# Rebuilding the opening of a fused recurrence and max-out kernel: block 0 transposed in fp32, weights in quarters, gate scale in the drive term, block 0's sums held open, TensorE warmed

## The chip, the cores and the metric

The kernel runs on one core of one Trainium2 chip. The metric is device microseconds of one execution; smaller is better. A run over 1.5% above the fastest of its kernel is called slow below, and kernels are compared by their fast runs. Times within a trace count from the start of its span, which is about 1.8 us shorter than the time of the run.

PE is TensorE, PEld its weight loads, DVE VectorE, ACT ScalarE, POOL GpSimd, SP SyncE (SPq its queue of DMA issues). A number like L381 is a line of that kernel's own source, so the same work has different line numbers in different kernels.

## The reference

```python
# x, f_logit: (4, 6144, 256); lower_bound: (256,); w1, w2: (256, 1024); w_out: (1024, 256)
sig = 1.0 / (1.0 + np.exp(-f_logit))
f = lower_bound + (1.0 - lower_bound) * sig
i = 1.0 - f
for t in range(S):                      # a recurrence over the sequence, per channel
    h = f[:, t] * h + i[:, t] * x[:, t]
    y[:, t] = h
tokens = y.reshape(B * S, D)            # 24576 x 256
out = np.maximum(tokens @ w1, tokens @ w2) @ w_out
```

Two identities matter. With om = 1 - lower_bound and u = sigmoid(-f_logit), i = om * u, and om is a constant of the channel. And max(a, b) = a + relu(b - a), so out = y @ (w1 @ w_out) + relu(y @ (w2 - w1)) @ w_out. The kernel calls w2 - w1 `wd` and w1 @ w_out `w13`.

## The kernel before

The 24576 tokens are worked in 48 blocks of 512. For each block f_logit and x are brought to channels-on-partitions, either by TensorE transposes (the first four blocks) or by a transposing DMA out of a bf16 scratch (all others, in chunks of two blocks: `fT`, `xT`). ACT makes u; DVE makes the decay ff, the drive v = u * x, and two scans of 512 columns, which give y. TensorE then does the first layer (16 matmuls of 512 columns with `wd`, each pair followed by a relu on ACT) and the second layer (40 matmuls of 256 columns: 8 with `w13`, 32 with `w_out`, called `wob`). In the loop the two layers of neighbouring blocks are interleaved. The part in question is what comes ahead of that loop:

```python
# block 0 comes in two halves of 256 tokens: cast to bf16, transpose, recurrence
        first_bf16(0, 0, nc.vector.tensor_copy)
        first_bf16(0, 1, nc.vector.tensor_copy)
        first_turn(0)
        first_recurrence(0)
        first_bf16(1, 0, nc.scalar.copy)
        first_bf16(1, 1, nc.scalar.copy)
        first_turn(1)
        first_recurrence(1)
        for fc in range(2):
            make_wd(fc, 1)          # w2 - w1 in fp32, then scaled by om into bf16
        make_wd(2, 2)
        pts = [turn_w1(0), turn_w1(1)]
        for fc in range(2):
            first_layer(0, fc)
        # ... (the rest of the first layer of block 0, w1 transposed for w13) ...
        make_w13()                  # scaled by om too: the scans run on u * x, without om
        turn(turn_steps(1))
        recurrence(1)               # gate, decays, drive, scans of block 1
        ahead("cross", cross, 4)
        for fc in range(FC):
            second_layer(0, fc)
        turn(turn_steps(2))
        gate(2)
        for fc in range(FC):
            first_layer(1, fc)
        for step in scan_steps(2):
            step()
        steps = turn_steps(3)
        turn(steps)
        if steps:
            gate(3)
        # ... the loop over blocks 2 to 47 ...

        def drive():                # for both halves of the channels at once
            xT = turned[j, 1]
            nc.vector.tensor_tensor(
                out=like(v[:, :, 0:nb], xT),
                in0=like(u[:, :, 0:nb], xT),
                in1=xT,
                op=ALU.mult,
            )
```

The weights are fetched in halves of 512 KB, w2 ahead of w1.

## Time and profile before

| | before |
|---|---|
| runs before the prediction, us | 402.15, 400.65, 424.38 |
| the profiled execution, us | 428.3 (a slow one) |
| first useful matmul of the weights, us | 11.2 |
| first layer of block 1 begins, us | 27.25 |
| a block in the loop, us | 7.82 |

How to read it: the profile that was there before the prediction is of a slow execution. The windows view tells what of it is the slow state. Its columns are the stretch, its length, then the busy time of PE, PEld, DVE, ACT and POOL with the number of instructions, the granted clock of TensorE, the DMA share and GB/s.

```profile
40.50:428.00 387.50, 360.19 (x2514) 273.36 (x2557) 219.89 (x312) 246.68 (x407) 18.55 (x39) 0.99 1.03 174
```

From 40.5 us on, TensorE worked 360.2 of 387.5 us. The waits view (who waited for whom: us in total, times, longest) says for what: the sigmoids waited 35.5 us for transposing DMAs.

```profile
ACT u L190 <- DMA fT<-scr_1_91: 18.2, 7, 4.6
ACT u L190 <- DMA fT<-scr_0_90: 17.3, 8, 5.2
```

40.5 + 360.2 = 400.7 us, which is within 2 us of the spans of the two later traces of this kernel outside the slow state (400.0 and 398.8 us). So a fast run has next to no stall in the loop, and only the opening offers time. Its timeline (start, duration, engine, line, operation, count, and in brackets the idle time just before with what ended it):

```profile
11.18 1.95 PE L352 MATMUL psO<-ident_f,w1n_110 128*128 128x128 f32 x8 [3.44 <-DMA w1n_110<-in_moe_w_dram]
12.93 3.62 PE L381 MATMUL dT<-y,wd 128*128 128x512 bf16 x8
...
17.63 1.89 PE L381 MATMUL dT<-y,wd 128*128 128x512 bf16 x7
...
21.75 1.02 ACT L190 ACTIVATE u<-tT 128x1024 bf16<-128x1024 bf16 x1
...
24.59 2.46 DVE L233 TENSOR_TENSOR_SCAN y<-ff,y,v 128x512 bf16<-128x512 bf16 x2
...
26.96 1.26 DVE L430 COPY osb<-psO 128x512 f32<-128x512 f32 x2
...
27.25 3.93 PE L381 MATMUL dT<-y,wd 128*128 128x512 bf16 x15
...
28.14 0.61 DVE L209 TENSOR_SCALAR ff<-u,nom 128x512 bf16<-128x512 bf16 x2
```

TensorE waits for the first half of w1 until 11.2 us. Its first eight first-layer matmuls run 0.43 us apart, the later ones 0.216. Block 1's first layer (L381 at 27.25) follows its scans (L233) directly.

### The profile page before, as it was taken

To read this page: it belongs to the slowest core of one execution; us is meant where nothing else is said; L and a number is where in the kernel's file an instruction comes from. 1 tells how busy PE (TensorE), PEld (TensorE's weight loads), DVE (VectorE), ACT (ScalarE), POOL (GpSimd) and SP (SyncE) were. 2 spreads that over 40 slices of the span, in tenths; PEclk is the share of its full clock that TensorE was granted. 3 is DMA by queue.
4 is the path that set the end of the run, shared out by engine and by line. 5 is a ranking of instruction groups with operands and counts; after the bars stand their busy time and mean duration, and the time that the engine had idled before them with its cause. 6 is when DMAs were issued, how large, how long until landed. Compare 5 with 4: busy or idle time off the path is not lost.

```text
span 428.3 us, 6970 instructions
## 1 busy us (share of the span) xinstructions
PE 392.8 (92%) x2744; PEld 296.8 (69%) x2792; DVE 248.7 (58%) x359; ACT 268.5 (63%) x447; POOL 26.4 (6%) x58
## 2 busy tenths in 40 slices
PE   3999979798789999998997899999998999999996
PEld 1677756576557777776775577767676777777775
DVE  5785637455357566564653557657547656567551
ACT  3656656557366676675673666756657676776762
POOL 1400000000000000000000000000000000000000
PEclk9999999999989999999999699999999999999999
DMA  7999999999999999999998999999999999998112
GB/s 245 222 220 198 123 157 141 137 169 252 81 240 226 119 239 233 112 248 168 183 237 75 218 158 186 250 145 170 219 131 231 226 216 164 268 157 179 79 69 100
DMA packets 103377, 77.01 MB, mean 180 GB/s; under 512 B 93552, under 2 KB 94064, under 8 KB 102640
## 3 DMA queue, kind: packets, MB, share of 16 engines
q1 hardware_dynamic: 100512, 51.13, 66.7%
q0 software_dynamic: 2544, 25.17, 36.1%
q8 instruction: 22, 0.36, 0.4%
q10 hardware_dynamic: 288, 0.26, 0.2%
q14 instruction: 11, 0.09, 0.1%
HBM read 53.48 MB, written 48.23 MB: 237 GB/s over the span
## 4 chain that ended last, share of the span: by engine, by line
PE 46%; DMA 34%; SPq 15%; ACT 3%; DVE 1%; issue 1%; ACTq 0%
PE psO L410 25%; DMA fT<-scr_0_90 20%; PE dT L381 19%; SPq L153 13%; DMA fT<-scr_1_91 12%; ACT u L190 2%; DMA w1n_110<-in_moe_w_dram 2%; SPq L433 1%; PE psO L352 1%; ACT rt L389 1%; PE tT L180 1%; PE psO L365 0%; SPq L121 0%; DVE osb L430 0%; DVE y L233 0%
## 5 line engine op out<-in xcount | busy, mean ns | idle before, releaser
L389 ACT ACTIVATE rt<-dT 128x512 bf16<-128x512 f32 x384 | 219.2, 598 | 104.1 <-PE dT L381 100.0
L381 PE MATMUL dT<-y,wd 128*128 128x512 bf16 x720 | 219.5, 384 | 21.3 <-ACT rt L389 19.5
L410 PE MATMUL psO<-wob,rt 128*128 128x256 bf16 x1536 | 230.7, 274 | 2.7 <-issue 0.4
L410 PEld LDWEIGHTS <-rt 128*128 128x128 bf16 x1536 | 170.7, 114 | 41.4 <-issue 1.1
L233 DVE TENSOR_TENSOR_SCAN y<-ff,y,v 128x512 bf16<-128x512 bf16 x88 | 107.9, 1268 | 0.1
L430 DVE COPY osb<-psO 128x512 f32<-128x512 f32 x94 | 64.7, 690 | 59.0 <-PE psO L410 58.9
L381 PEld LDWEIGHTS <-wd 128*128 128x128 bf16 x768 | 75.8, 99 | 33.2 <-issue 24.6
L209 DVE TENSOR_SCALAR ff<-u,nom 128x512 bf16<-128x512 bf16 x94 | 29.0, 351 | 105.0 <-ACT u L190 105.0
L410 PE MATMUL psO<-w_109,y 128*128 128x256 bf16 x384 | 74.0, 275 | 0.0
L410 PEld LDWEIGHTS <-y 128*128 128x128 bf16 x384 | 43.4, 113 | 42.6 <-issue 3.5
L190 ACT ACTIVATE u<-fT 128x1024 bf16<-128x1024 bf16 x44 | 46.4, 1054 | 35.5 <-DMA fT<-scr_1_91 18.2
L220 DVE TENSOR_TENSOR v<-u,xT 128x1024 bf16<-128x1024 bf16 x44 | 30.3, 688 | 3.8 <-DMA xT<-scr_0_92 1.8
L98 POOL DMA_DIRECT2D scr_0_90<-in_f_logit_dram x11 | 5.4, 493 | 149.7 <-DMA fT<-scr_0_90 149.7
L98 POOL DMA_DIRECT2D scr_1_91<-in_f_logit_dram x11 | 5.3, 486 | 148.8 <-DMA fT<-scr_1_91 148.1
L233 DVE TENSOR_TENSOR_SCAN y<-ff,v 128x512 bf16<-128x512 bf16 x6 | 7.0, 1208 | 0.0
L98 POOL DMA_DIRECT2D scr_0_92<-in_x_dram x11 | 5.4, 488 | 18.7 <-DMA xT<-scr_0_92 16.9
L98 POOL DMA_DIRECT2D scr_1_93<-in_x_dram x11 | 5.3, 486 | 15.7 <-DMA xT<-scr_1_93 14.9
L190 ACT ACTIVATE u<-tT 128x1024 bf16<-128x1024 bf16 x3 | 3.2, 1058 | 4.3 <-PE tT L180 4.3
L352 PE MATMUL psO<-ident_f,w1n_110 128*128 128x128 f32 x8 | 1.9, 422 | 3.4 <-DMA w1n_110<-in_moe_w_dram 3.4
L341 ACT ACTIVATE wd<-wdf,om 128x128 bf16<-128x128 f32 (+1 forms) x6 | 2.2, 428 | 4.3 <-DVE wdf L333 4.3
L352 PEld LDWEIGHTS psO<-ident_f,w1n_110 128*128 128x128 f32 x8 | 1.6, 221 | 3.7 <-issue 3.7
L220 DVE TENSOR_TENSOR v<-u,tT 128x1024 bf16<-128x1024 bf16 x3 | 3.6, 1216 | 0.0
(49 smaller groups left out, 45.1 us busy)
## 6 DMA issues: line engine op xcount, KB each, us to landing
out_dram<-osb SPq DMA_DIRECT2D x47, 512.0 KB, 4.8
scr_0_90<-in_f_logit_dram POOLq DMA_DIRECT2D x11, 512.0 KB, 7.5
scr_0_92<-in_x_dram POOLq DMA_DIRECT2D x11, 512.0 KB, 12.4
scr_1_91<-in_f_logit_dram POOLq DMA_DIRECT2D x11, 512.0 KB, 7.9
scr_1_93<-in_x_dram POOLq DMA_DIRECT2D x11, 512.0 KB, 13.6
fn<-in_f_logit_dram POOLq DMA_DIRECT2D x3, 256.0 KB, 7.9
xn<-in_x_dram POOLq DMA_DIRECT2D x3, 256.0 KB, 8.6
w2n_112<-in_moe_w_dram SPq DMA_DIRECT2D x1, 512.0 KB, 6.5
```

The source lines that it names most:

```text
L98: nc.gpsimd.dma_start(out=scr[0:nt, :].rearrange("(p i) d -> p (i d)", p=P), in_=src.rearrange("(p i) d -> p (i d)", p=P),)
L153: nc.sync.dma_start_transpose(out=dst[:, :, 0:nt], in_=held[c, s][0:nt, :])
L180: nc.tensor.transpose(dst, src, ident[:])
L190: nc.scalar.activation(out=like(u[:, :, 0:nb], fT), in_=fT, func=AF.Sigmoid, scale=-1.0)
L209: nc.vector.tensor_scalar(out=ff[:, h, 0:nb], in0=u[:, h, 0:nb], scalar1=nom[:, h : h + 1], scalar2=1.0, op0=ALU.mult, op1=ALU.add,)
L220: nc.vector.tensor_tensor(out=like(v[:, :, 0:nb], xT), in0=like(u[:, :, 0:nb], xT), in1=xT, op=ALU.mult,)
L233: nc.vector.tensor_tensor_scan(out=y[:, h, 0:nb], data0=ff[:, h, 0:nb], data1=v[:, h, 0:nb], initial=init, op0=ALU.mult, op1=ALU.add,)
L352: nc.tensor.transpose(pt[:, kc, q, :], half(w1n, g)[:, kc, 2 * r + q], ident_f[:])
L381: nc.tensor.matmul(dT[:, 0:nb], lhsT=wd[:, kc, fc * P : (fc + 1) * P], rhs=y[:, kc, 0:nb], start=(kc == 0), stop=(kc == KC - 1),)
L389: nc.scalar.activation(out=rt[:, 0:nb], in_=dT[:, 0:nb], func=AF.Relu)
L410: nc.tensor.matmul(ps[:, r, :], lhsT=left, rhs=right, start=(s == 0 and (r == 0 or j == NBLK - 1)), stop=(s == n - 1 and (r == 1 or j == N ...
L430: nc.vector.tensor_copy(out=osb[:, 2 * g : 2 * g + 2, :], in_=ps[:])
```

## The change

Its intent is to start TensorE earlier and keep it fed:

- block 0's fp32 halves are transposed without the casts to bf16; block 0's decays move from DVE to ACT, and some of its relus from ACT to DVE;
- the weights come in quarters, w1 ahead of w2, so that the first layer can begin on a quarter;
- om goes into the drive (one scaled product for each half of the channels), so `wd` and `w13` need no scaling;
- block 0's second layer begins with the `w_out` part, as soon as its relus are there, and its sums stay open in PSUM until `w13` is ready (`second_first`, `second_last`);
- eight matmuls on a constant are to bring TensorE to its full rate sooner and keep it there (the kernel before had eight small transposes for this);
- half of block 1's second layer is interleaved with block 2's first layer.

The core of the diff (cut):

```diff
-        def drive():
+        def drive(h):
             xT = turned[j, 1]
-            nc.vector.tensor_tensor(
-                out=like(v[:, :, 0:nb], xT),
-                in0=like(u[:, :, 0:nb], xT),
-                in1=xT,
-                op=ALU.mult,
-            )
+            scaled_product(v[:, h, 0:nb], xT[:, h], u[:, h, 0:nb], h)   # x * om * u
...
         return [
             lambda: decay(0),
+            lambda: drive(0),
+            lambda: scan(0),
             lambda: decay(1),
-            drive,
-            lambda: scan(0),
+            lambda: drive(1),
             lambda: scan(1),
         ]
...
-    NG = 2
+    NG = 4
...
+        keep_warm(5)
+        first_turn(0, 0)
+        first_gate(0)
+        first_turn(0, 1)
+        first_drive(0)
+        keep_warm(1)
+        turn_w1(0)
+        first_scan(0, 0)
+        make_wd(0)
+        first_scan(0, 1)
...
+        keep_w1T(1, nc.vector.tensor_copy)
+        keep_w1T(2, nc.scalar.copy)
+        second_first(range(4))
+        keep_w1T(3, nc.vector.tensor_copy)
+        t1 = turn_steps(1)
+        turn(t1[: len(t1) // 2])
+        gate(1)
+        second_first(range(4, 6))
+        turn(t1[len(t1) // 2 :])
+        for step in scan_steps(1):
+            step()
+        second_first(range(6, 8))
         make_w13()
-        turn(turn_steps(1))
-        recurrence(1)
+        turn(turn_steps(2))
+        gate(2)
         ahead("cross", cross, 4)
         for fc in range(FC):
-            second_layer(0, fc)
-        turn(turn_steps(2))
-        gate(2)
-        for fc in range(FC):
             first_layer(1, fc)
+            second_last(fc)
         for step in scan_steps(2):
             step()
         steps = turn_steps(3)
         turn(steps)
-        if steps:
-            gate(3)
+        gate(3)
...
```

More of the change, by code (lines that the diff above doesn't have):

```diff
@@ L115, with fetch_first, first_turn @@
     raws = {}
-    def fetch_first(k):
-        nt = TB // 2
-        for s in range(2):
-            raw = const.tile([P, nt // P, D], FP32, name=f"raw{k}{s}")
-            nc.sync.dma_start(
-                out=raw[:],
-                in_=srcs[s][0, k * nt : (k + 1) * nt, :].rearrange(
-                    "(p i) d -> p i d", p=P
-                ),
-            )
-            raws[k, s] = raw
-    def first_bf16(k, s, copy):
-        raw = raws[k, s]
-        nat = const.tile([P, raw.shape[1], D], BF16, name=f"nat{k}{s}")
-        copy(out=nat[:], in_=raw[:])
-        raws[k, s] = nat
-    def first_turn(k):
-        nt = TB // 2
-        for s in range(2):
-            dst = ps_t.tile([P, KC, nt // P, P], BF16, name="tT")
-            for q in range(nt // P):
-                for h in range(KC):
-                    nc.tensor.transpose(
-                        dst[:, h, q, :],
-                        raws[k, s][:, q, h * P : (h + 1) * P],
-                        ident[:],
-                    )
-            raws[k, s] = dst[:].rearrange("p k i m -> p k m i")
+    HB = TB // 2
+    def fetch_first(k, s):
+        raw = const.tile([P, HB // P, D], FP32, name=f"raw{k}{s}")
+        nc.sync.dma_start(
+            out=raw[:],
+            in_=srcs[s][0, k * HB : (k + 1) * HB, :].rearrange(
+                "(p i) d -> p i d", p=P
+            ),
+        )
+        raws[k, s] = raw
+    def first_turn(k, s):
+        dst = ps_t.tile([P, KC, HB // P, P], FP32, name="tT")
+        for q in range(HB // P):
+            for h in range(KC):
+                nc.tensor.transpose(
+                    dst[:, h, q, :],
+                    raws[k, s][:, q, h * P : (h + 1) * P],
+                    ident_f[:],
+                )
+        raws[k, s] = dst[:].rearrange("p k i m -> p k m i")
     def cross(c):
@@ L195, in like, with scaled_product @@
     def like(t, src):
-        if len(src.shape) == 3:
+        if len(src.shape) == len(t.shape):
             return t
+        if len(t.shape) == 2:
+            return t.rearrange("p (m i) -> p m i", m=P)
         return t.rearrange("p k (m i) -> p k m i", m=P)
+    def scaled_product(out, xT, u, h):
+        nc.vector.scalar_tensor_tensor(
+            out=like(out, xT),
+            in0=xT,
+            scalar=om[:, h : h + 1],
+            in1=like(u, xT),
+            op0=ALU.mult,
+            op1=ALU.mult,
+        )
     def scan_steps(j):
@@ L216, in decay @@
             )
-        def drive():
+        def drive(h):
             xT = turned[j, 1]
-            nc.vector.tensor_tensor(
-                out=like(v[:, :, 0:nb], xT),
-                in0=like(u[:, :, 0:nb], xT),
-                in1=xT,
-                op=ALU.mult,
-            )
+            scaled_product(v[:, h, 0:nb], xT[:, h], u[:, h, 0:nb], h)
         def scan(h):
@@ L250, with first_gate @@
     first = {}
-    def first_recurrence(k):
-        nt = TB // 2
-        cols = slice(k * nt, (k + 1) * nt)
+    def first_gate(k):
+        cols = slice(k * HB, (k + 1) * HB)
         if k == 0:
@@ L258, in first_recurrence @@
             ys[0] = ypool.tile([P, KC, TB], BF16, name="y")
-        u, ff, v, y = (*(first[t] for t in ("u", "ff", "v")), ys[0])
-        fT, xT = raws[k, 0], raws[k, 1]
+        u, ff = first["u"], first["ff"]
+        fT = raws[k, 0]
         nc.scalar.activation(
@@ L264, in first_recurrence, with first_drive, first_scan @@
         for h in range(KC):
-            nc.vector.tensor_scalar(
+            nc.scalar.activation(
                 out=ff[:, h, cols],
-                in0=u[:, h, cols],
-                scalar1=nom[:, h : h + 1],
-                scalar2=1.0,
-                op0=ALU.mult,
-                op1=ALU.add,
-            )
-        nc.vector.tensor_tensor(
-            out=like(v[:, :, cols], xT), in0=like(u[:, :, cols], xT), in1=xT,
-            op=ALU.mult,
-        )
-        for h in range(KC):
-            nc.vector.tensor_tensor_scan(
-                out=y[:, h, cols],
-                data0=ff[:, h, cols],
-                data1=v[:, h, cols],
-                initial=y[:, h, nt - 1 : nt] if k else 0.0,
-                op0=ALU.mult,
-                op1=ALU.add,
-            )
-    def recurrence(j):
-        gate(j)
-        for step in scan_steps(j):
-            step()
+                in_=u[:, h, cols],
+                func=AF.Identity,
+                bias=one[:],
+                scale=nom[:, h : h + 1],
+            )
+    def first_drive(k):
+        cols = slice(k * HB, (k + 1) * HB)
+        for h in range(KC):
+            scaled_product(
+                first["v"][:, h, cols], raws[k, 1][:, h], first["u"][:, h, cols], h
+            )
+    def first_scan(k, h):
+        cols = slice(k * HB, (k + 1) * HB)
+        y = ys[0]
+        nc.vector.tensor_tensor_scan(
+            out=y[:, h, cols],
+            data0=first["ff"][:, h, cols],
+            data1=first["v"][:, h, cols],
+            initial=y[:, h, HB - 1 : HB] if k else 0.0,
+            op0=ALU.mult,
+            op1=ALU.add,
+        )
     ident_f = const.tile([P, P], FP32)
@@ L298 @@
     waited = const.tile([P, 1], FP32)
+    one = const.tile([P, 1], FP32)
+    heat = const.tile([P, TB], BF16)
     warm = const.tile([P, 1], FP32)
     wob = wpool.tile([P, FC, D], BF16)
-    wdf = wpool.tile([P, KC, DFF], FP32)
     wd = wpool.tile([P, KC, DFF], BF16)
@@ L308, with by_unit @@
     w2n = [wpool.tile([P, KC, NQ * P], FP32, name=f"w2n{g}") for g in range(NG)]
-    def half(w, g):
-        return w[g][:].rearrange("p kc (m q) -> p kc q m", q=NQ)
-    def fcs(w, kc, g):
-        return w[:, kc, g * NQ * P : (g + 1) * NQ * P].rearrange(
-            "p (q m) -> p q m", q=NQ
-        )
+    def by_unit(w):
+        return w[:].rearrange("p kc (m q) -> p kc q m", q=NQ)
     def fetch_w(g):
-        cols = slice(g * DFF // NG, (g + 1) * DFF // NG)
-        for w, src in ((w2n, moe_w2), (w1n, moe_w1)):
+        cols = slice(g * NQ * P, (g + 1) * NQ * P)
+        for w, src in ((w1n, moe_w1), (w2n, moe_w2)):
             nc.sync.dma_start(
@@ L324, in fetch_w, with fetch_wo @@
             )
+    def fetch_wo(g, n):
+        rows = slice(g * NQ * P, (g + n) * NQ * P)
+        nc.gpsimd.dma_start(
+            out=wob[:, g * NQ : (g + n) * NQ, :].rearrange(
+                "p (g q) c -> p g (q c)", g=n
+            ),
+            in_=moe_w_out[rows, :].rearrange("(g p q) c -> p g (q c)", g=n, q=NQ),
+        )
     def pool_waits(t):
         nc.gpsimd.tensor_copy(out=waited[:], in_=t)
-    def make_wd(fc, n):
-        g, r = divmod(fc, NQ)
-        qs = slice(r, r + n)
-        cols = slice(fc * P, (fc + n) * P)
-        nc.vector.tensor_tensor(
-            out=wdf[:, :, cols].rearrange("p kc (q m) -> p kc q m", q=n),
-            in0=half(w2n, g)[:, :, qs],
-            in1=half(w1n, g)[:, :, qs],
-            op=ALU.subtract,
-        )
-        for kc in range(KC):
-            if g == 0:
-                nc.scalar.mul(wd[:, kc, cols], wdf[:, kc, cols], om[:, kc : kc + 1])
-            else:
-                nc.vector.tensor_scalar_mul(
-                    out=wd[:, kc, cols], in0=wdf[:, kc, cols], scalar1=om[:, kc : kc + 1]
-                )
@@ L347, in turn_w1, with make_wd @@
-    def turn_w1(k):
-        g, r = divmod(k, NQ // 2)
-        pt = ps_o.tile([P, KC, 2, P], FP32, name="psO")
-        for kc in range(KC):
-            for q in range(2):
-                nc.tensor.transpose(
-                    pt[:, kc, q, :], half(w1n, g)[:, kc, 2 * r + q], ident_f[:]
-                )
-        return pt
-    def keep_w1T(k, pt):
-        dst = w1T[:, 2 * k : 2 * k + 2, :].rearrange("p q (k d) -> p k q d", k=KC)
-        nc.vector.tensor_copy(out=dst, in_=pt[:])
-    def make_w13():
-        for kc in range(KC):
-            psw = ps_o.tile([P, 2, D], FP32, name="psO")
+    def make_wd(g):
+        for kc in range(KC):
+            nc.vector.tensor_tensor(
+                out=wd[:, kc, g * NQ * P : (g + 1) * NQ * P].rearrange(
+                    "p (q m) -> p q m", q=NQ
+                ),
+                in0=by_unit(w2n[g])[:, kc],
+                in1=by_unit(w1n[g])[:, kc],
+                op=ALU.subtract,
+            )
@@ new lines, with turn_w1, keep_w1T, make_w13 @@
+    w1ps = {}
+    def turn_w1(g):
+        pt = ps_o.tile([P, KC, NQ, P], FP32, name="psO")
+        for kc in range(KC):
+            for q in range(NQ):
+                nc.tensor.transpose(
+                    pt[:, kc, q, :], by_unit(w1n[g])[:, kc, q], ident_f[:]
+                )
+        w1ps[g] = pt
+    def keep_w1T(g, copy):
+        dst = w1T[:, NQ * g : NQ * (g + 1), :].rearrange("p q (k d) -> p k q d", k=KC)
+        copy(out=dst, in_=w1ps[g][:])
+    def make_w13():
+        psw = ps_o.tile([P, 2, D], FP32, name="psO")
+        for kc in range(KC):
@@ L364, in make_w13 @@
             for fc in range(FC):
                 nc.tensor.matmul(
-                    psw[:, 0, :],
+                    psw[:, kc, :],
                     lhsT=w1T[:, fc, kc * P : (kc + 1) * P],
                     rhs=wob[:, fc, :],
-                    start=(fc == 0),
-                    stop=(fc == FC - 1),
+                    start=(kc == 0 and fc == 0),
+                    stop=(kc == KC - 1 and fc == FC - 1),
+                    skip_group_check=True,
                 )
-            nc.scalar.mul(w13[:, kc, :], psw[:, 0, :], om[:, kc : kc + 1])
+        nc.scalar.copy(out=w13[:], in_=psw[:])
@@ L374, with relu_act, relu_dve, first_layer @@
     rts = {}
-    def first_layer(j, fc):
-        nb = blocks[j][2]
+    def relu_act(out, in_):
+        nc.scalar.activation(out=out, in_=in_, func=AF.Relu)
+    def relu_dve(out, in_):
+        nc.vector.tensor_scalar_max(out=out, in0=in_, scalar1=0.0)
+    def first_layer(j, fc, relu=relu_act, c0=0, c1=TB):
         y = ys[j]
@@ L381, in first_layer @@
             nc.tensor.matmul(
-                dT[:, 0:nb],
+                dT[:, c0:c1],
                 lhsT=wd[:, kc, fc * P : (fc + 1) * P],
-                rhs=y[:, kc, 0:nb],
+                rhs=y[:, kc, c0:c1],
                 start=(kc == 0),
@@ L387, in first_layer, with second_first, second_last, second_layer @@
             )
-        rt = rpool.tile([P, TB], BF16, name="rt")
-        nc.scalar.activation(out=rt[:, 0:nb], in_=dT[:, 0:nb], func=AF.Relu)
-        rts[j, fc] = rt
+        if c0 == 0:
+            rts[j, fc] = rpool.tile([P, TB], BF16, name="rt")
+        relu(rts[j, fc][:, c0:c1], dT[:, c0:c1])
     acc = {}
-    def second_layer(j, slot):
+    psf = {}
+    def second_first(fcs):
+        ns = TB // P
+        for i in range(ns):
+            g, r = divmod(i, 2)
+            for fc in fcs:
+                if r == 0 and fc == 0:
+                    psf[g] = ps_o.tile([P, 2, D], FP32, name="psO")
+                nc.tensor.matmul(
+                    psf[g][:, r, :],
+                    lhsT=rts[0, fc][:, i:TB:ns],
+                    rhs=wob[:, fc, :],
+                    start=(r == 0 and fc == 0),
+                    stop=False,
+                    skip_group_check=True,
+                )
+    def second_last(k):
+        ns = TB // P
+        i, kc = divmod(k, KC)
+        g, r = divmod(i, 2)
+        if k == 0:
+            psf["osb"] = opool.tile([P, TB // P, D], FP32, name="osb")
+        osb = psf["osb"]
+        nc.tensor.matmul(
+            psf[g][:, r, :],
+            lhsT=ys[0][:, kc, i:TB:ns],
+            rhs=w13[:, kc, :],
+            start=False,
+            stop=(r == 1 and kc == KC - 1),
+            skip_group_check=True,
+        )
+        if r == 1 and kc == KC - 1:
+            nc.vector.tensor_copy(out=osb[:, 2 * g : 2 * g + 2, :], in_=psf[g][:])
+            if g == 1:
+                nc.sync.dma_start(
+                    out=out[0:TB, :].rearrange("(p n) d -> p n d", p=P), in_=osb[:]
+                )
+    def second_layer(j, slot, nslot=FC):
         b, t0, nb, c, o = blocks[j]
@@ L399, in second_layer @@
         total = ns * n
-        for k in range(slot * total // FC, (slot + 1) * total // FC):
+        for k in range(slot * total // nslot, (slot + 1) * total // nslot):
             i, s = divmod(k, n)
@@ L447 @@
     with tc.manual_schedule():
-        nc.sync.dma_start(out=lbc[:], in_=lower_bound.rearrange("(h p) -> p h", p=P))
+        nc.vector.memset(heat[:], 1.0)
+        nc.vector.memset(one[:], 1.0)
+        fetch_first(0, 0)
+        fetch_first(0, 1)
+        nc.scalar.dma_start(
+            out=lbc[:], in_=lower_bound.rearrange("(h p) -> p h", p=P)
+        )
+        fetch_w(0)
+        fetch_first(1, 0)
+        fetch_first(1, 1)
+        for g in range(1, NG):
+            fetch_w(g)
+        nc.scalar.activation(out=warm[:], in_=one[:], func=AF.Sigmoid)
         nc.vector.tensor_copy(out=ident[:], in_=ident_f[:])
@@ L453 @@
         nc.vector.tensor_scalar_add(out=nom[:], in0=lbc[:], scalar1=-1.0)
-        fetch_first(0)
-        fetch_first(1)
-        for g in range(NG):
-            fetch_w(g)
-        pool_waits(w2n[0][:, 0, 0:1])
-        nc.gpsimd.dma_start(
-            out=wob[:].rearrange("p (g q) c -> p g (q c)", g=NG),
-            in_=moe_w_out.rearrange("(g p q) c -> p g (q c)", g=NG, q=NQ),
-        )
+        pool_waits(w2n[1][:, 0, 0:1])
+        fetch_wo(0, 2)
+        fetch_wo(2, 1)
         done["fetch"] = done["cross"] = 1
+        ahead("fetch", fetch, 1)
@@ L464 @@
+        fetch_wo(3, 1)
         ahead("fetch", fetch, 4)
-        nc.scalar.activation(out=warm[:], in_=om[:, 0:1], func=AF.Sigmoid)
-        wt = ps_d.tile([P, TB], BF16, name="dT")
-        for q in range(8):
-            nc.tensor.transpose(wt[:, 0:P], ident[:], ident[:])
-        first_bf16(0, 0, nc.vector.tensor_copy)
-        first_bf16(0, 1, nc.vector.tensor_copy)
-        first_turn(0)
-        first_recurrence(0)
-        first_bf16(1, 0, nc.scalar.copy)
-        first_bf16(1, 1, nc.scalar.copy)
@@ L475 @@
-        first_turn(1)
-        first_recurrence(1)
-        for fc in range(2):
-            make_wd(fc, 1)
-        make_wd(2, 2)
-        pts = [turn_w1(0), turn_w1(1)]
-        for fc in range(2):
-            first_layer(0, fc)
-        for k in range(2):
-            keep_w1T(k, pts[k])
-        for fc in range(2, 4):
-            first_layer(0, fc)
-        make_wd(4, 2)
-        make_wd(6, 2)
-        pts = [turn_w1(2), turn_w1(3)]
-        for fc in range(4, 8):
-            first_layer(0, fc)
@@ L492, with keep_warm @@
-        for k in range(2):
-            keep_w1T(2 + k, pts[k])
+        wt = ps_d.tile([P, TB], FP32, name="dT")
+        def keep_warm(n):
+            for _ in range(n):
+                nc.tensor.matmul(
+                    wt[:], lhsT=heat[:, 0:P], rhs=heat[:], start=True, stop=True
+                )
+        keep_warm(5)
[7 more added lines that the diff above has]
+        make_wd(0)
@@ new lines @@
+        first_scan(0, 1)
+        first_turn(1, 0)
+        first_gate(1)
+        first_turn(1, 1)
+        keep_warm(2)
+        first_drive(1)
+        first_layer(0, 0, relu_act, 0, HB)
+        first_layer(0, 1, relu_act, 0, HB)
+        first_scan(1, 0)
+        make_wd(1)
+        first_scan(1, 1)
+        turn_w1(1)
+        first_layer(0, 2, relu_act, 0, HB)
+        first_layer(0, 3, relu_act, 0, HB)
+        turn_w1(2)
+        first_layer(0, 0, relu_act, HB, TB)
+        first_layer(0, 1, relu_dve, HB, TB)
@@ new lines @@
+        make_wd(2)
+        first_layer(0, 2, relu_act, HB, TB)
+        first_layer(0, 3, relu_dve, HB, TB)
+        keep_w1T(0, nc.vector.tensor_copy)
+        first_layer(0, 4, relu_act)
+        make_wd(3)
+        first_layer(0, 5, relu_dve)
+        turn_w1(3)
+        first_layer(0, 6, relu_act)
+        first_layer(0, 7, relu_dve)
+        keep_w1T(1, nc.vector.tensor_copy)
[3 more added lines that the diff above has]
+        t1 = turn_steps(1)
@@ L520 @@
             if j == 2:
-                if 0 in gates:
-                    gate(gates.pop(0))
-                early = scan_steps(j + 1)
-                for fc in range(FC):
-                    second_layer(1, fc)
-                    if fc < 4:
-                        early[fc]()
-                early[4]()
+                for slot in range(FC // 2):
+                    second_layer(1, slot)
             for fc in range(FC):
@@ L533 @@
                     second_layer(j - 1, fc)
+                else:
+                    second_layer(1, FC + fc, 2 * FC)
                 n = len(steps)
@@ L537 @@
                     gate(gates[fc])
-                if fc == 0 and 2 < j < NBLK - 1:
+                if fc == 0 and j < NBLK - 1:
                     scans = scan_steps(j + 1)
```

## The prediction

> **What bounds the kernel now.** Two regimes. In the steady part TensorE sets the pace: the timeline shows one 512-token block every 7.82 us, with 16 matmuls of 512 columns (0.216 us apart) and 40 of 256 (0.109 us). The profiled execution (428.3 us) was a slow one: the windows show only 360.2 us of PE work in the 387.5 us after 40.5, and the waits show ACT idle 35.5 us for transposing DMAs (fT). 40.5 + 360.2 = 400.7 us, just the fast runs (400.65, 402.15); so a fast run has almost no stall after 40.5 us, and a saving must come out of the opening.
>
> **The opening now (timeline).** PE does 22.6 us of warm work by 36.3 us, so about 13.7 us are lost: first useful work at 11.2 us (chain: 7.4 us wait for the first half of w1), then eight first-layer matmuls of block 0 at 0.43 us instead of 0.216 (1.7 us lost). Block 1's first layer starts at 27.2 us: block 1 transposed 21.1-22.2, sigmoid to 22.8, decays, drive (1.22 us), two scans to 27.05.
>
> **What the change does.** Gone: four casts (0.43 us on DVE, 0.62 on ACT), six scalings of the weight difference (0.35-0.5 us), decays of block 0 from DVE to ACT. PE is warmed by five matmuls (5 x 0.43 = 2.1 us). The Trainium skill (TensorE: Matmul & The Clock Gate, Part 1) wants about 3.4 us of sustained activity before full rate; the trace agrees (half rate from 12.9 to 16.5 us, full after it), so five alone may be too few, but PE is not the limit here. Weights come in quarters: the first pair should land near 6.3 us instead of 11.0, the last near 13.3 instead of 13.7: bytes are the same, so the weights' end hardly moves.
>
> Then VectorE limits. Between about 5.7 us and the release of the second w1-transpose buffer (which the held-open sums of block 0 need) it has, in order: two drives (0.7), four scans (0.7), four weight differences (about 1.0, from 0.62 for 256 strided fp32 elements before), four relus (0.4-0.68), two copies (0.68): about 13 us, nearly gapless, ending near 18.7 us. From there: second layer 1.7, transposes 0.5, sigmoid 1.2, scans of block 1 4.3: first layer of block 1 near 26.6 instead of 27.2. Block 0's sums already done but for eight matmuls (cost 0.4, interleaved); halves of block 1's second layer interleaved with block 2's first layer, which today is paced by the relus (0.5 us each): gains 0.8. Net gain about 1 us (0 to 4).
>
> In the loop the drive becomes two operations of 512 at about 0.6 us instead of one of 0.69: 0.5 us more DVE per block. By the timeline scans end 1.1 us before the next block needs them, and the new order no longer puts the copy of a sum ahead of the first scan: hidden in fast runs. In slow runs each late fT then costs about 0.5 us more.
>
> **Predicted:** 400.2 us, 8 in 10 between 395.5 and 406. Faster by over 2%: 0.05; within 2%: 0.88; slower: 0.07.
>
> **What would show it.** Steps right if: first-layer matmuls of block 0 start before 9 us; the sums of block 0 start at 17-20 us, waiting for a DVE copy; first layer of block 1 at 25-27 us; block period still 7.82 us; drive near 0.6 us each.
>
> **What would make it wrong.** Weight differences at 0.35 us instead: sums start at 16.5 and the gain is 3 us. The transposing DMAs not moving forward with PE (block 4's fT landed at 36.9 us, xT at 40.1, barely before use): gain lost. The drive slower than 0.7 us: a stall every block. More slow executions (one of three runs before was 424): a median near 420.

## The result

| | before | after |
|---|---|---|
| median of 4 runs, us | 401.61 | 402.17 |
| runs, us | 402.15, 400.65, 424.38, 401.06 | 402.42, 402.04, 402.30, 402.01 |
| ratio of the fast runs | | 1.0021 (95%: 1.0000 to 1.0041) |

A ratio is the mean time of one kernel's fast runs over that of the other's of the same rounds, so it is not quite the ratio of the medians. Later, beside other runs of before, the kernel after gave 1.0030 (1.0016 to 1.0044): it is about 1 us slower. The rebuilt opening brought nothing at the end.

The profile after is of a fast run (span 400.5 us, clock 1.00). Its timeline, with the lines that answer to those of before (L349 w1 transposes, L384 first layer, L406 block 0's held-open sums, L181 sigmoid, L231 scan, L431 copy of block 0's sums, L171 transposes, L212 decay):

```profile
9.26 0.60 PE L384 MATMUL dT<-y,wd 128*128 128x256 bf16 x4
9.70 0.64 PE L349 MATMUL psO<-ident_f,w1n 128*128 128x128 f32 x4
...
17.21 1.91 PE L406 MATMUL psO<-wob,rt 128*128 128x256 bf16 x16 [0.73 <-ACT w1T L356]
...
19.60 1.02 ACT L181 ACTIVATE u<-tT 128x1024 bf16<-128x1024 bf16 x1 [2.44 <-PE tT L171]
...
23.94 1.28 DVE L231 TENSOR_TENSOR_SCAN y<-ff,y,v 128x512 bf16<-128x512 bf16 x1
...
24.04 1.02 ACT L181 ACTIVATE u<-tT 128x1024 bf16<-128x1024 bf16 x1
...
25.27 0.38 PE L384 MATMUL dT<-y,wd 128*128 128x512 bf16 x1 [0.62 <-DVE y L231]
...
27.42 0.69 DVE L431 COPY osb<-psO 128x512 f32<-128x512 f32 x1 [2.20 <-PE psO L422]
...
29.38 0.61 PE L171 MATMUL tT<-ident,fn 128*128 128x128 bf16 x8
29.58 0.69 DVE L431 COPY osb<-psO 128x512 f32<-128x512 f32 x1 [1.47 <-PE psO L422]
...
30.19 0.34 DVE L212 TENSOR_SCALAR ff<-u,nom 128x512 bf16<-128x512 bf16 x1
...
31.15 0.61 PE L171 MATMUL tT<-ident,xn 128*128 128x128 bf16 x8 [1.16 <-ACT u L181]
...
32.67 0.75 DVE L194 SCALAR_TENSOR_TENSOR v<-tT,om,u 128x512 bf16<-128x512 bf16 x1
...
34.79 0.38 PE L384 MATMUL dT<-y,wd 128*128 128x512 bf16 x1 [0.63 <-DVE y L231]
...
41.19 0.59 PE L384 MATMUL dT<-y,wd 128*128 128x512 bf16 x2
```

At 25.27 us the first layer of block 1 is running, two microseconds ahead of the slow trace of before. Then DVE waits 2.20 and 1.47 us for block 0's sums, with block 2's decays queued behind the copies although block 2's sigmoid had ended at 25.06. TensorE pays for that twice: 1.16 us at block 3's transposes and 0.63 us at block 2's first layer. The second wait is for block 2's scan itself. The first is put down to a sigmoid on ACT, and DVE stands behind it by way of a buffer. There are two buffers `tT` for transposed blocks, and block 2's x keeps one of them until its second drive (32.67 us). Building the two kernels shows the rest: block 3's x is put into the buffer of block 3's own f, which is free only after the sigmoid that reads it (30.08 to 31.10 us), while in e10, below, it gets the buffer of block 2's x. The last line of the timeline, the second first-layer pair of block 3, is the mark used below: from there on all kernels do the same work.

The chain of waits that ended last then runs without a stall; three of its pieces (start, us, what), one block apart each, and the last group:

```profile
372.01 0.71 PE psO L453 x5
379.83 0.71 PE psO L453 x5
387.65 0.71 PE psO L453 x5
391.73 4.93 PE psO L453 x45
```

7.82 us a block, as before. The groups view (busy us, mean ns of one, then idle before) gives the two drives of the loop, first before, then after:

```profile
L220 DVE TENSOR_TENSOR v<-u,xT 128x1024 bf16<-128x1024 bf16 x44 | 30.3, 688 | 3.8 <-DMA xT<-scr_0_92 1.8
```

```profile
L194 DVE SCALAR_TENSOR_TENSOR v<-xT,om,u 128x512 bf16<-128x512 bf16 x88 | 65.6, 746 | 0.0
```

The scaled product takes 746 ns for half of the columns that the plain one did in 688 ns: 0.80 us more DVE per block.

### The profile page after: what moved, and what is told of

Same layout as the page of the kernel before. It is cut to its first block, busy times and chain, and to the rows that moved or that the text cites. A ratio compares the mean times of both kernels' runs of the same rounds, so it can differ in the third digit from the quotient of the medians.

```text
span 400.5 us, 7047 instructions
## 1 busy us (share of the span) xinstructions
PE 386.5 (96%) x2752; PEld 295.6 (74%) x2800; DVE 283.7 (71%) x406; ACT 269.0 (67%) x443; POOL 27.5 (7%) x60
## 4 chain that ended last, share of the span: by engine, by line
PE 92%; DVE 3%; DMA 1%; issue 1%; ACT 1%; SPq 0%; DVEq 0%
PE psO L453 53%; PE dT L384 38%; DVE y L231 1%; DMA raw<-in_f_logit_dram 1%; DVE v L194 1%; PE psO L406 0%; DVE wd L334 0%; PE tT L132 0%; PE psO L349 0%; DVE ff L212 0%; ACT u L181 0%; SPq L315 0%; PE psO L422 0%; SPq L120 0%; DVE osb L431 0%
## 5 line engine op out<-in xcount | busy, mean ns | idle before, releaser
L375 ACT ACTIVATE rt<-dT 128x512 bf16<-128x512 f32 (+1 forms) x384 | 222.3, 593 | 113.6 <-PE dT L384 113.3
L384 PE MATMUL dT<-y,wd 128*128 128x512 bf16 (+1 forms) x728 | 217.7, 377 | 2.6 <-DVE y L231 1.3
L231 DVE TENSOR_TENSOR_SCAN y<-ff,y,v 128x512 bf16<-128x512 bf16 x88 | 113.0, 1284 | 3.1
L384 PEld LDWEIGHTS <-wd 128*128 128x128 bf16 x776 | 75.7, 98 | 7.7 <-DVE wd L334 1.8
L212 DVE TENSOR_SCALAR ff<-u,nom 128x512 bf16<-128x512 bf16 x94 | 32.7, 348 | 62.8 <-ACT u L181 62.8
L453 PE MATMUL psO<-w,y 128*128 128x256 bf16 x376 | 71.8, 273 | 0.0
L194 DVE SCALAR_TENSOR_TENSOR v<-xT,om,u 128x512 bf16<-128x512 bf16 x88 | 65.6, 746 | 0.0
L181 ACT ACTIVATE u<-fT 128x1024 bf16<-128x1024 bf16 x44 | 46.2, 1050 | 0.0
L98 POOL DMA_DIRECT2D scr<-in_f_logit_dram x22 | 10.9, 494 | 259.0 <-DMA fT<-scr 258.3
L98 POOL DMA_DIRECT2D scr<-in_x_dram x22 | 10.7, 489 | 36.2 <-DMA xT<-scr 34.3
L194 DVE SCALAR_TENSOR_TENSOR v<-tT,om,u 128x512 bf16<-128x512 bf16 (+1 forms) x10 | 6.2, 639 | 1.8 <-ACT u L259 1.5
L231 DVE TENSOR_TENSOR_SCAN y<-ff,v 128x512 bf16<-128x512 bf16 x6 | 7.3, 1223 | 0.2
L181 ACT ACTIVATE u<-tT 128x1024 bf16<-128x1024 bf16 x3 | 3.1, 1024 | 2.4 <-PE tT L171 2.4
L521 PE MATMUL dT<-heat 128*128 128x512 bf16 x8 | 3.3, 535 | 1.5 <-DVE one L492 1.5
L406 PE MATMUL psO<-wob,rt 128*128 128x256 bf16 x32 | 4.0, 272 | 0.7 <-ACT w1T L356 0.7
L406 PEld LDWEIGHTS <-rt 128*128 128x128 bf16 x32 | 3.4, 114 | 1.1 <-issue 1.0
```

What stands on the lines that cost most here:

```text
L98: nc.gpsimd.dma_start(out=scr[0:nt, :].rearrange("(p i) d -> p (i d)", p=P), in_=src.rearrange("(p i) d -> p (i d)", p=P),)
L181: nc.scalar.activation(out=like(u[:, :, 0:nb], fT), in_=fT, func=AF.Sigmoid, scale=-1.0)
L194: nc.vector.scalar_tensor_tensor(out=like(out, xT), in0=xT, scalar=om[:, h : h + 1], in1=like(u, xT), op0=ALU.mult, op1=ALU.mult,)
L212: nc.vector.tensor_scalar(out=ff[:, h, 0:nb], in0=u[:, h, 0:nb], scalar1=nom[:, h : h + 1], scalar2=1.0, op0=ALU.mult, op1=ALU.add,)
L231: nc.vector.tensor_tensor_scan(out=y[:, h, 0:nb], data0=ff[:, h, 0:nb], data1=v[:, h, 0:nb], initial=init, op0=ALU.mult, op1=ALU.add,)
L375: nc.scalar.activation(out=out, in_=in_, func=AF.Relu)
```

## The experiments

Theory G: the opening gains two microseconds by block 1 and gives them back before block 3, because block 2's scans stand behind the copies of block 0's sums. Rival L: the longer drive costs in the loop. Rival S: the slow trace showed too slow an opening, and a fast run of before opens faster.

All runs gave correct results. Their marks, next to those of the two kernels (us; "mark" is the second first-layer pair of block 3, "last group" the start of the last group of the chain):

| trace | first layer of block 1 | mark | last group | last group - mark |
|---|---|---|---|---|
| before, fast (e1) | 27.14 | 40.87 | 391.41 | 350.54 |
| before, fast (e9) | 25.96 | 39.69 | 390.23 | 350.54 |
| after | 25.27 | 41.19 | 391.73 | 350.54 |
| after (e8) | 25.16 | 41.08 | 391.62 | 350.54 |
| e3 | 25.36 | 39.16 | 389.70 | 350.54 |
| e4 | 25.20 | 41.12 | 391.66 | 350.54 |
| e5 | 26.11 | 39.83 | 390.37 | 350.54 |
| e7 | 24.73 | 38.74 | 390.24 | 351.50 |
| e10 (= e2) | 24.82 | 38.62 | 389.16 | 350.54 |

One caution for the first column: in the rows after, e8, e3, e4 and e10 it is the second matmul, which waits for the second scan, and in the rows of before, e5 and e7 it is the first. The second matmul of those starts 0.22 us later (27.36 us in e1, 26.18 in e9, 24.94 in e7), and where two kernels are compared below, second matmuls are.

### e1_before_again: the kernel before, unchanged

> The kernel before, unchanged, only to get a trace of it in the fast state (its first trace was of a slow execution, 428.3 us). Theory G (the opening's gain is given back between 25 and 40 us): the fast trace opens like the slow one (first layer of block 1 at 27.2 us within 0.5, first layer of block 3 at 40.2 us within 0.5), and has a block every 7.82 us after that without a stall; span about 399.5 to 400.5. Rival S (the slow trace showed too slow an opening): first layer of block 1 a microsecond or more before 27.2 us.

Measured: 401.87 us, span 400.0. As a single run its state is on record as unknown; its time and its clock (0.999) are those of a fast run. The timeline and the end of the chain:

```profile
11.43 1.95 PE L352 MATMUL psO<-ident_f,w1n 128*128 128x128 f32 x8 [3.46 <-DMA w1n<-in_moe_w_dram]
...
27.14 3.93 PE L381 MATMUL dT<-y,wd 128*128 128x512 bf16 x16
...
30.91 0.61 PE L180 MATMUL tT<-ident,fn 128*128 128x128 bf16 x8
...
31.80 0.38 PE L410 MATMUL psO<-w,y 128*128 128x256 bf16 x2
...
36.17 4.32 PE L381 MATMUL dT<-y,wd 128*128 128x512 bf16 x18
...
40.87 0.59 PE L381 MATMUL dT<-y,wd 128*128 128x512 bf16 x2
```

```profile
391.41 4.93 PE psO L410 x45
```

The opening is that of the slow trace within 0.3 us, so S is not borne out by this trace (e9, below, opens 1.2 us earlier). The kernel after leads by 2.09 us at block 1 (25.27 against 27.36) and trails by 0.32 us at the mark (41.19 against 40.87). It is still 0.32 us behind at the last group: the whole difference arises before the mark.

### e2_scan2_early: block 2's scans ahead of the copies

```diff
+        for step in scan_steps(2):
+            step()
         for fc in range(FC):
             first_layer(1, fc)
             second_last(fc)
-        for step in scan_steps(2):
-            step()
```

> The kernel after, with the decays, drives and scans of block 2 put ahead of the two copies of block 0's sums on VectorE. Theory G: in the kernel after, VectorE stood idle 3.7 us for those copies (waits of 2.20 and 1.47 us) with block 2's scans behind them, and TensorE paid 1.16 us (transposes of block 3) and 0.63 us (first layer of block 2). With the scans first, both waits go: first layer of block 3 near 38.4 us instead of 40.2, time 1.8 us less than the kernel after (about 400.4), ratio to before about 0.998. Rival L (the longer drive in the loop costs the microsecond): no change from the kernel after, 402.2.

Measured: fast runs 400.97, 399.99, 399.98 and 399.88 us, two slow ones (442.26 and 450.27); ratio 0.9979 (0.9966 to 0.9992).

### e10_scan2_again: the same kernel once more

> e2 once more, for more fast runs and a trace in the fast state: fast runs 399.8 to 401.0, ratio to before 0.997 to 0.999; in the trace the transposes of block 3 follow each other with no wait for ACT, the first layer of block 2 waits for no scan, and the second first-layer pair of block 3 starts near 38.9 us (41.19 in the kernel after).

Measured: fast runs 399.73, 399.89, 400.84, 399.84 and 400.72 us, one slow (429.58); ratio 0.9977 (0.9954 to 1.0001). Its profile is of a fast run; timeline, then the end of the chain:

```profile
24.82 0.38 PE L384 MATMUL dT<-y,wd 128*128 128x512 bf16 x1 [0.62 <-DVE y L231]
...
27.93 1.28 DVE L231 TENSOR_TENSOR_SCAN y<-ff,y,v 128x512 bf16<-128x512 bf16 x1
...
29.13 1.26 DVE L431 COPY osb<-psO 128x512 f32<-128x512 f32 x2
...
29.38 0.61 PE L171 MATMUL tT<-ident,xn 128*128 128x128 bf16 x8
...
38.62 0.59 PE L384 MATMUL dT<-y,wd 128*128 128x512 bf16 x2
```

```profile
389.16 4.93 PE psO L453 x45
```

Both waits are gone: block 2's scans end at 29.2 us (34.7 in the kernel after), and block 3's x is transposed at 29.38 with no idle time before it. From the first layer of block 1 to the mark this kernel takes 13.80 us (38.62 - 24.82), the kernel before 13.51 (40.87 - 27.36), the kernel after 15.92 (41.19 - 25.27). The trace of e2, a slow run but not yet disturbed here, gives 13.80 too (38.88 - 25.08). The 2.12 us by which the kernel after exceeds e10 are the two waits, counted from start to start: 8 transposes take 0.45 us, so those of x could have begun at 29.83 instead of 31.15 (1.32 us), and two matmuls stand 0.216 us apart, but 33.78 and 34.79 did (0.79 us). The fast runs of e2 and e10 together average 400.2 us, those of after 402.1 (both batches): 1.9 us. Theory G holds, and moving six instructions turns the change into one that is a little faster than before, by about 0.2% (clear of no difference in the rounds of e2, just not in those of e10).

### e3_scan2_t1_early: block 1's f transposed earlier

```diff
-        second_first(range(4))
         keep_w1T(3, nc.vector.tensor_copy)
         t1 = turn_steps(1)
         turn(t1[: len(t1) // 2])
         gate(1)
+        second_first(range(4))
         second_first(range(4, 6))
         turn(t1[len(t1) // 2 :])
```

(on top of e2)

> e2, and block 1's f transposed (and its sigmoid begun) before the first 16 matmuls of block 0's held-open sums instead of after them. The block-1 f landed at about 17.2 us, so the sigmoid should start near 17.9 instead of 19.6 us. Theory G: first layer of block 1 about 1 us earlier (24.2 instead of 25.3, then TensorE is the limit), time about 399.4, ratio to before about 0.995. Rival (DMA sets the pace of the opening, or gives the gain back at block 4, whose xT landed at 40.6 us): first layer of block 1 earlier but time no better than e2.

Measured: 400.33, 399.75, 401.12, 399.94, 402.75 and 401.66 us; ratio 0.9997 (0.9975 to 1.0019). The expectation was missed. The sigmoid did start at 17.95 us, but block 1's x was transposed only at 20.36, and DVE waited 1.66 us for it; the first layer of block 1 came at 25.36, no earlier than in the kernel after. The traced run is as fast as e2. Why three other runs took 0.8 to 2.4 us longer than the traced one, no trace shows.

### e7_t1_all_early: block 1's x earlier as well

```diff
         second_first(range(4))
+        turn(t1[len(t1) // 2 :])
         second_first(range(4, 6))
-        turn(t1[len(t1) // 2 :])
```

(on top of e3)

> e3 with block 1's x transposed straight after the first 16 matmuls of the held-open sums too (in e3 VectorE waited 1.66 us for it). Theory G: the drive of block 1 starts near 19.9 us instead of 21.0, first layer of block 1 near 24.3 instead of 25.3, first layer of block 3 about 0.9 us earlier than in e3 (37.3), time near 399.2. Rival (the transposing DMAs of block 4, landed at 38.7 and 40.3 us in e3, now come too late): first layer of block 1 earlier, but a wait at block 4 and no gain over e2.

Measured: fast runs 400.77, 401.94, 399.40 and 400.28 us, two slow (440.25, 439.14); ratio 0.9994 (0.9968 to 1.0019). The timeline:

```profile
17.69 0.62 PE L171 MATMUL tT<-ident,fn 128*128 128x128 bf16 x8 [1.66 <-DMA fn<-in_f_logit_dram]
...
24.73 0.59 PE L384 MATMUL dT<-y,wd 128*128 128x512 bf16 x2
...
38.74 0.59 PE L384 MATMUL dT<-y,wd 128*128 128x512 bf16 x2
...
55.96 1.06 ACT L181 ACTIVATE u<-fT 128x1024 bf16<-128x1024 bf16 x1 [1.27 <-DMA fT<-scr]
```

Again no gain over e2: the second matmul of block 1's first layer comes at 24.94 us, against 24.82 in e10. The trace shows two reasons. TensorE now waits 1.66 us for block 1's f_logit to land (17.69 us), where the other order had matmuls to do. And at block 6 the sigmoid waits 1.27 us for its transposing DMA, which the table shows as 0.96 us between the mark and the last group. The rival was right that DMA costs time in this trace, though at block 6 and not at block 4. The other runs were not traced; one of them, at 399.40 us, is the fastest of all.

### e4_no_warm: without the warming matmuls

```diff
-        keep_warm(5)
...
-        keep_warm(1)
...
-        keep_warm(2)
```

(on top of the kernel after; the call of `keep_warm(2)` was left in with 0)

> The kernel after without its eight warming matmuls. If warming matters to the end time: TensorE stays at half rate[...], so the first layer of block 0 (256 columns 0.21 us apart instead of 0.109) and the w1 transposes slow down and the sums of block 0 start up to 1 us later, time 402.2 to 403.2. If VectorE and the landing of the weights set the opening: within 0.3 us of the kernel after.

Measured: 402.24, 402.45, 402.52, 402.20 and 402.72 us; ratio 1.0036 (1.0022 to 1.0049), where the kernel after had 1.0021 and 1.0030 with intervals that overlap it. The times that were expected overlap as well, so the trace has to decide: the mark is at 41.12 us, against 41.19 and 41.08 in the two traces of the kernel after. The warming moves nothing there. TensorE reached full rate without it; the first fp32 transposes of block 0 and the second ones, without warming:

```profile
4.23 2.06 PE L132 MATMUL tT<-ident_f,raw 128*128 128x128 f32 x8 [4.23 <-DMA raw<-in_f_logit_dram]
...
7.39 1.32 PE L132 MATMUL tT<-ident_f,raw 128*128 128x128 f32 x8 [0.25 <-DMA raw<-in_f_logit_dram]
...
9.17 0.49 PE L384 MATMUL dT<-y,wd 128*128 128x256 bf16 x3 [0.35 <-DVE y L281]
```

and in the kernel after, with warming:

```profile
4.28 1.55 PE L132 MATMUL tT<-ident_f,raw 128*128 128x128 f32 x8 [0.50 <-DMA raw<-in_f_logit_dram]
...
7.67 1.32 PE L132 MATMUL tT<-ident_f,raw 128*128 128x128 f32 x8 [1.04 <-DMA raw<-in_f_logit_dram]
```

The first eight are 0.5 us slower without warming. The second eight took the same 1.32 us by chance, as the starts of single transposes in the traces show. Without warming they stand 0.213 us apart until 6.7 us and 0.11 us apart from about 7.8 us on, the third of the second eight; with warming there is a wait among the second eight (8.03 to 8.37 us). With warming the spacing halves at about 5.2 us in this trace, but in e8, the same kernel, only at about 8.0 us. The marks of the two are 0.11 us apart all the same.

### e5_scale_in_drive: one part of the change on the kernel before

```diff
-            drive,
+            lambda: drive(0),
+            lambda: drive(1),
...
-            out=wdf[:, :, cols].rearrange("p kc (q m) -> p kc q m", q=n),
+            out=wd[:, :, cols].rearrange("p kc (q m) -> p kc q m", q=n),
...
-            if g == 0:
-                nc.scalar.mul(wd[:, kc, cols], wdf[:, kc, cols], om[:, kc : kc + 1])
-            else:
-                nc.vector.tensor_scalar_mul(...)
...
-            nc.scalar.mul(w13[:, kc, :], psw[:, 0, :], om[:, kc : kc + 1])
+            nc.scalar.copy(out=w13[:, kc, :], in_=psw[:, 0, :])
```

> The kernel before with one part of the change alone: the gate scale in the drive term (two scaled products of 512 columns, about 0.75 us each, for one product of 0.69 us), and so no scaling of the weight difference or of w13. Theory G: TensorE in the kernel before works without a gap from 11.4 us, and the scans end about 1 us before they are needed, so neither the shorter making of the weights nor the longer drive reaches the end time: ratio to before 0.999 to 1.001, a block still every 7.82 us. Rival L (the longer drive costs in the loop): ratio 1.002 or more.

Measured: fast runs 401.13, 400.78, 400.21 and 401.25 us, two slow (428.12, 431.64); ratio 1.0000 (0.9985 to 1.0015). (The order of the steps stays that of before, both decays first; the kernel after, with its own order, has the same 350.54 us.) L falls: with the drive of the change, the stretch from the mark to the last group is 350.54 us, as it is without it. The same number stands in the table for eight of nine traces.

The trace is 1.04 us ahead of e1 at the mark (39.83 against 40.87). This need not be the change: the first half of w1 had landed earlier, with the first w1 transposes at 10.08 instead of 11.43 us, although the fetches are the same. e9 was made to see whether that is so.

### e9_before_third: how much of before's opening hangs on w1

> A second trace of the kernel before, to see how much of its opening hangs on when the first half of w1 lands (11.4 us in the first fast trace, whose run took 401.87 us; 10.1 us in the trace of e5, which fetches the same in the same order and was 1.0 us ahead at block 3). If the landing of w1 shifts the whole run: time minus 401.87 equals the shift of the first w1 transpose from 11.43 us, within 0.3 us, in a fast run.

Measured: 400.60 us. The timeline and the end of the chain:

```profile
10.13 1.95 PE L352 MATMUL psO<-ident_f,w1n 128*128 128x128 f32 x8 [2.22 <-DMA w1n<-in_moe_w_dram]
...
39.69 0.59 PE L381 MATMUL dT<-y,wd 128*128 128x512 bf16 x2
```

```profile
390.23 4.93 PE psO L410 x45
```

w1 was 1.30 us earlier than in e1 and the run 1.27 us shorter. From the first w1 transposes to block 1's first layer it is 15.71 us in e1, 15.83 in e9 and 16.07 in the slow trace, although the spacing of TensorE's matmuls halved at different moments (about 16.5, 13.1 and 17.1 us). So in the kernel before the landing of the first half of w1 passes on to the end, and it varies. That it explains all the spread of before's fast runs (400.5 to 402.3 us) is not shown: only these two were traced, and on different chips. Against e1 the kernel after loses 0.3 us, against e9 1.6 us (402.18 in e8 against 400.60), and the mean of before's fast runs, 401.1, lies in between. The lead at block 1 depends on it too: against e9 it is 0.91 us (25.27 against 26.18) and not 2.09, so that S was right in part.

### e6_sums_not_held: e2 without the held-open sums

```diff
-        second_first(range(4))
         keep_w1T(3, nc.vector.tensor_copy)
...
-        second_first(range(4, 6))
...
-        second_first(range(6, 8))
         make_w13()
+        turn(turn_steps(1))
+        gate(1)
+        for step in scan_steps(1):
+            step()
+        ahead("cross", cross, 4)
+        for fc in range(FC):
+            second_layer(0, fc)
         turn(turn_steps(2))
         gate(2)
-        ahead("cross", cross, 4)
-        for step in scan_steps(2):
-            step()
         for fc in range(FC):
             first_layer(1, fc)
-            second_last(fc)
+        for step in scan_steps(2):
+            step()
```

(and the last quarter of `w_out` fetched ahead of block 1)

> e2 with block 0's sums not held open: w1 times w_out first, then block 1's transposes, then all 40 matmuls of block 0's second layer, then block 2's transposes and block 1's first layer, as in the kernel before; the last quarter of w_out is fetched ahead of block 1. If holding the sums open brings what the change meant it to: first layer of block 1 near 26.2 us instead of 25.3, first layer of block 3 near 38.7 instead of 37.9 to 38.2, time about 0.8 us over e2 (400.7). If it brings nothing: equal to e2 (399.9).

Measured: fast runs 400.50, 400.38, 400.74, 400.51 and 400.48 us, one slow (439.19); ratio 0.9992 (0.9978 to 1.0005). That is 0.3 us above the mean of e2 and e10, within the reach of the intervals; 0.8 was expected. Its trace is of the slow run, but its opening shows no wait for a transposing DMA: the mark is at 39.34 us, against 38.62. So holding the sums open is worth 0.3 us by the runs and 0.7 by the marks of two traces, and not clearly more than nothing; either holds only once the scans stand ahead of the copies. As the change had it, the copies that it put there cost 2.1 us. The quarters, the fp32 transposes and the decays on ACT were not tested one by one.

### e8_after_again: the kernel after beside the others

> The kernel after, unchanged, on the same chip and beside the same runs of before as the other three, to compare with: 402.0 to 402.4, ratio to before 1.002 to 1.003.

Measured: 402.18, 402.22, 401.95, 402.25, 401.95 and 401.92 us; ratio 1.0030 (1.0016 to 1.0044). The waits are there again (1.16 us at block 3's transposes, 0.64 us at block 2's first layer).

### Slow runs

Besides e1 and e9, slow were 12 of 40 runs of before, none of 10 of after, 3 of 12 of e2 and e10 together, none of 6 of e3 and of 5 of e4, 2 of 6 of e5, 1 of 6 of e6, 2 of 6 of e7. In the slow traces the sigmoids wait for transposing DMAs in the loop (35.5 us in the first trace of before, 34.7 in e2's, 33.2 in e6's). What sets this state off was not studied; the counts are too small, and the runs too unlike in their batches, to say that a kernel prevents it.

## Why the prediction was right, and which of its terms were wrong

The forecast was a time within 2%, 400.2 us with 395.5 to 406 as its range; measured were 402.2. The class and the range held. The sign of the small net gain did not: a gain of about 1 us was expected, and a loss of about 1 us came. A range of 10 us holds either, so that it was met says little for the steps, and part of it is luck.

- **That the loop does not change: right.** 7.82 us a block, and 350.54 us from the mark to the last group with the old drive and the new one. The drive was mis-sized: 0.746 us measured for "about 0.6". The margin was as well. I read 1.1 us between the end of the scans and their use in the slow trace of before; in e1 the scans end at 54.89 us (52.44 + 2.45) and the next block's first layer begins at 55.54, which is 0.65 us. In the kernel after a block's second scan ends at 55.45 us (54.17 + 1.28) and the next block's first layer begins at 55.85. That is 0.4 us. It sufficed, so the "stall every block" that was feared of a drive over 0.7 us did not come.
- **That the opening was bound by DVE: right, and a little quicker than said.** The weight differences took 0.75 us a quarter and not 1.0. The w1T copies, which release the buffers of the held-open sums, ended at 18.4 us, and the sums began at 17.2 us (17 to 20 was said). They waited for a copy on ACT, not for one on DVE. The first layer of block 0 began at 9.26 us (8.97 in e8), where "before 9 us" was said.
- **Block 1's first layer: better than said.** 25.27 us in place of 26.6.
- **The step that failed is what was to follow**: "Block 0's sums already done but for eight matmuls (cost 0.4, interleaved); halves of block 1's second layer interleaved with block 2's first layer, which today is paced by the relus (0.5 us each): gains 0.8." The cost of the eight matmuls was near: from block 1's first layer to block 3's transposes 4.11 us (29.38 - 25.27), against 3.55 before (30.91 - 27.36), which makes 0.56 us. But I took TensorE to go on without a stall there, and did not follow DVE's order past block 1. The copies at the end of these sums stand on DVE ahead of block 2's scans, and TensorE lost 2.11 us by it. The interleaving was mis-sized too: from the start of block 1's second layer to the mark it takes 8.80 us in e10 (38.62 - 29.82) and 9.07 in e1 (40.87 - 31.80), so its gain, as far as two kernels that differ in more can show it, is 0.27 us and not 0.8.
- **The base was not fixed.** The kernel before was taken as one number, and its opening hangs on the landing of w1: two traced runs differ by 1.27 us, with landings 1.30 us apart. The changed kernel gave fast runs within 0.5 us of each other, near the slow end of before's.
- **The warm-up: right that it would not matter,** and the remark that five matmuls may be too few fits one trace of two. TensorE was at full rate from about 5.2 us in one trace of the kernel after and from about 8.0 in the other, and from about 7.8 us in e4 without any.
- **Of the other ways to lose that were named,** more slow executions did not show in the kernel after (none of 10), and neither did late transposing DMAs (no sigmoid waited for one). Such a DMA did show in e7, at block 6, once the opening was made earlier still.

## What to carry to other kernels

When work is moved forward on one engine, follow the in-order queues of the others past the place where the gain is made: the gain here was real at block 1 (0.9 to 2.1 us), and two copies placed ahead of the next block's scans gave it all back by block 3. Compare two traces by one common mark and by the time from there to the end; if that time is equal to the hundredth, as here, the whole difference lies ahead of the mark. And look how far the kernel before scatters through one DMA landing, before asking where one microsecond went.

## What the Trainium skill lacked or had wrong

- "TensorE: Matmul & The Clock Gate", Part 4, says that full rate does not engage for transposes, which would not count as busy in the same way. Here it did: in e4 TensorE did nothing but fp32 transposes until 8.55 us, and these stood 0.213 us apart until 6.7 us and 0.11 us apart from about 7.8 us on. The bf16 transposes stood 0.107 us apart at 4.6 to 7.7 us in e1 and 0.056 us apart at 26.5 us, in the midst of other matmuls; whether they alone bring full rate was not tested.
- The same page, Part 1, gives about 3.4 us of sustained activity before full rate. The traces agree with it in size only. The transposes of e4 began at 4.23 us and the faster ones at about 7.8, 3.6 us later. In the kernel before it was 5.1 us in e1 (11.43 to about 16.5) and 5.9 us in the slow trace (11.18 to about 17.1), counted from the first w1 transpose.
- "VectorE: DVE Perf Modes", the perf-mode tier table, has no row for a product of two tensors and a per-channel scalar (scalar_tensor_tensor). Here it took 746 ns for 512 bf16 columns in SBUF, where the plain tensor_tensor took 688 ns for 1024: more than twice per column. It has no row for tensor_tensor_scan either, which took 1284 ns for 512.
- No page has the two states of a kernel on one core with many transposing DMAs: 401 us, or 410 to 450 us with the sigmoids waiting for those DMAs (35.5 us in one trace).
